# Linear attention and a squared-ReLU MLP on one core: the order of loads at the opening, and products, sums and sends at the very end

## The chip, the cores and the metric

The kernel runs on one core of a Trainium2 chip. The metric is the device time of one execution in microseconds, given as the median of several; lower is better. The profile shows one execution, whose span (first to last instruction) is a few microseconds shorter than the time.

The engines are named as the profile names them: PE is TensorE (PEld its weight loads), DVE is VectorE, ACT is ScalarE, POOL is GpSimd, SP is SyncE, which here only issues transfers. Each engine carries out its own instructions in the order in which the program emits them, and waits for other engines through semaphores.

## The reference

Linear attention over 8 batches, 8 heads, 576 positions and 64 features, then a two-layer MLP on the 4608 x 512 result:

```python
kv = np.einsum('bhsd,bhse->bhde', k, v)
out = np.einsum('bhsd,bhde->bhse', q, kv)
rms = np.sqrt(np.mean(out * out, axis=-1, keepdims=True) + 1e-06)
x = (out / rms * g_norm)          # then (B,H,S,D) -> (B*S, H*D)
h = x @ w_in                      # 512 -> 2048
r = np.maximum(h, 0.0)
return (r * r) @ w_out            # 2048 -> 512
```

q, k and v are float32. The two weight matrices come in 64 bits, and the kernel makes float32 of them itself.

## The kernel before

**Tiles and strips.** The 4608 rows of x are 36 tiles of 128 tokens; four tiles make a strip, so there are nine strips (s = 0 to 8). Each strip goes through an up-projection (`up_first` in strip 0, `up` later) and a down-projection (`down` in strips 0 and 1, `down_deep` from strip 2 on). From strip 1 on the matrix products are done by a scheme of seven products instead of eight on 2 x 2 blocks; `down_deep` uses it twice, so that each of its seven products p (in the order 4, 1, 2, 6, 5, 7, 3) is made of seven small products j.

**Attention as slices.** The attention of each batch is cut into small steps, the list `slices` (L487 to L512). `attend(n)` (L515) emits the steps up to number n; the main loop (L784 to L844) calls it between the MLP's products. So the attention of later batches is interleaved with the products of earlier strips, and only batch 0's first four tiles have to be done before anything else. That is the opening.

**The opening.** Heads go in pairs p = 0 to 3. For one pair the steps are: `convert_on_act(p)` (L199), the part of the conversion of a piece of W_in that runs on ACT (L203, L206); `transposed_query` (L318: four PE transposes L331, copied by ACT L333); `key_value` (L342: twenty matmuls L349, copied by ACT at L351 and L352); `first_queries(p)` (L415: the matmuls q times kv at L419, two DVE steps of the conversion of piece p, then `mean_squares`: ACT squares L384, DVE sums L386, L387); `first_normalized(p)` (L425: the third conversion step, the square root on ACT L392, DVE's reciprocal and one Newton step L393 to L398, the product x_n L430, the fourth conversion step); `first_features(p)` (L436: four PE transposes of x_n at L440, copied into xT by ACT at L441). `conversion` (L209) is the DVE part of a piece: four instructions, L215, L217, L221 and L224. Pair p's normalization and features follow pair p+1's queries and keys in the list. At the end of the opening `attend(ready[0] - 2)` (L780) emits all but the last pair's `first_normalized` and `first_features`; two more pieces, 4 and 5, then get their ACT part (L781, L782); then the main loop emits the last two steps.

All PSUM tiles of the attention come from one pool of four slots (`apsum`, L90).

**Loads of the opening.** All go from SP's queue in the order of L298 to L302: the rests of k and v, then in turn head pair p (k, v, and two transfers of q) and piece p of W_in (512 KB), then pieces up to the eighth. A piece is one of 32 parts of the two weight matrices (16 of W_in, 16 of W_out); pieces 0 to 3 hold the columns that strip 0 needs first. Eight buffers hold raw pieces; a buffer is loaded again when its piece has been converted. The rest of the conversion runs beside strip 0's up-projection (L588): `convert` (L280) emits the conversion of two pieces at a time, and ACT's part runs two pieces ahead.

**The end of a strip.** In `down_deep(s, k, i)` (L756), `small_products` (L723) emits the small products of product p: j = 1, 2, 3 for i = 0 and 4 to 7 for i = 1, each eight matmuls (L734). `PLACE` (L721) says to which of two PSUM tiles, and where in it, j is added: 1, 2 and 6 in the first; 5, 7, 3 and 4 in the second. `together(s, p)` (L739) makes the four quarters of p's result: an ACT copy of product 1 (L746), then four DVE sums (L745 is their line), then, for p = 2, 7 and 3, the sum with an earlier part and the sending of a finished block. It is emitted within the next product's steps, and for the last product (k = 6) at the very end. `send` (L652) sends a block of 256 tokens by 256 columns: two tiles, and for each of them the row groups of `out_rows` (L521). For batches from 2 on, a tile's 32-row groups go to rows that lie apart, so a tile takes four transfers, and a block eight, all from SP (L655).

Of the kernel before, what the change touches and what calls it, by code (L numbers as in the profile page):

```python
# [1 line left out]

# [17 lines left out]
def kernel(  # L20
# [34 lines left out]
    nc = tc.nc  # L55
    P = 128
    B, H, S, D = q.shape
# [3 lines left out]
    NP = H // 2  # L61
    FC = d_ff // P
    C = S // P
    REST = S - C * P
    PAIR = 2 * C + 1
    assert 2 * REST == P
    N_TILE = n_tok // P
    NT = 4
    STRIP = NT * P
    TH = STRIP // 2  # L70
    N_STRIP = N_TILE // NT
    DEEP = 2
    SQ = 32
    Q_ON_PE = 2
# [9 lines left out]
    small = ctx.enter_context(tc.tile_pool(name="small", bufs=3))  # L84
# [77 lines left out]
    def load_next(q_eng=nc.sync):  # L162
        u = next(to_load, None)
        if u is not None:
            load(*u, q_eng)


    KH, FH, DH = NP // 2, d_ff // 2, d_model // 2
    FQ = FC // 2
# [3 lines left out]
    w_in = wpool.tile([P, KH, NG, 7, WN // 2], FP32, name="w_in")  # L173
# [35 lines left out]
    def conversion(i, dest):  # L209

        c, r, high = words.pop(i)
        ci = c.bitcast(I32)


        yield nc.vector.tensor_scalar(out=c, in0=c, scalar1=LEAST, scalar2=MOST, op0=ALU.max, op1=ALU.min)  # L215

        yield nc.vector.tensor_scalar(  # L217
            out=ci, in0=ci, scalar1=3, scalar2=0x3FFFFFFF, op0=ALU.logical_shift_left, op1=ALU.bitwise_and
        )

        yield nc.vector.scalar_tensor_tensor(  # L221
            out=ci, in0=high, scalar=-(2**30), in1=ci, op0=ALU.bitwise_and, op1=ALU.bitwise_or
        )
        yield nc.vector.tensor_tensor(out=dest.bitcast(I32), in0=ci, in1=r, op=ALU.add)  # L224
# [69 lines left out]
    one = const.tile([P, 1], FP32, name="one")  # L294
# [1 line left out]
    nc.scalar.sqrt(one, one)  # L296

    load_rest(0, nc.sync)  # L298
    for p in range(NP):
        load_next()  # L300
        load_piece()
    load_more(0)  # L302
# [7 lines left out]
    flat = lambda t: t.rearrange("p h d -> p (h d)")  # L310
# [70 lines left out]
    def mean_squares(ps):  # L381
        n = ps.shape[-1] // D
        sq = xn_pool.tile([P, d_model], FP32, name="sq", tag="sq", bufs=1)
        nc.scalar.activation(sq, ps, AF.Square)  # L384
        ms = small.tile([P, H], FP32, name="ms", tag="ms")
        nc.vector.reduce_sum(out=ms, in_=by_head(sq), axis=AX.X)  # L386
        nc.vector.tensor_scalar(out=ms, in0=ms, scalar1=1.0 / D, scalar2=EPS, op0=ALU.mult, op1=ALU.add)  # L387
        return ms
# [23 lines left out]

    first = {}

    def first_queries(p):  # L415

        ps = apsum.tile([P, NT, P], FP32, name="x_ps", tag="at")
        for n in range(NT):
            nc.tensor.matmul(ps[:, n, :], lhsT=qT[0, p][:, n, :], rhs=kvd[0, p], start=True, stop=True)  # L419
        steps = conversion(p, w_in[:, p % KH, 0, p // KH * 2 : p // KH * 2 + 2])  # L420
        next(steps)
        next(steps)
        first[p] = flat(ps), mean_squares(flat(ps)), steps

    def first_normalized(p):  # L425
        ps, ms, steps = first.pop(p)
        next(steps)
        x_n["first", p] = t = xn_pool.tile([P, NT, P], FP32, name="x_n", tag="x_n")
        r = inverse_root(ms)
        nc.vector.tensor_tensor(  # L430
            out=by_head(flat(t)), in0=by_head(ps), in1=r.unsqueeze(2).to_broadcast([P, H, D]), op=ALU.mult
        )
        for _ in steps:
            pass

    def first_features(p):  # L436
        t, x = x_n.pop(("first", p)), open_xt(0)
# [47 lines left out]
        minus(nc.vector, t4, x(1, 0), t2)  # L485

    slices, ready = [], {}  # L487
    for b in range(B):
        for p in range(NP):
            if b:  # L490
                slices += [(transposed_query, (b, p)), (key_value, (b, p))]
                continue

            slices += [(convert_on_act, (p,)), (transposed_query, (b, p)), (key_value, (b, p))]
            if p > 0:
                slices.append((first_normalized, (p - 1,)))
            slices.append((first_queries, (p,)))
            if p > 0:
                slices.append((first_features, (p - 1,)))
        first_n = b // 2 * PAIR + (C if b % 2 else 0)  # L500
        ns = list(range(first_n, first_n + C + b % 2))
        if b == 0:
            slices += [(first_normalized, (NP - 1,)), (first_features, (NP - 1,))]
            ready[0] = len(slices)
            continue
        for i in range(len(ns) + 1):
            if i < len(ns):
                slices.append((query, (ns[i],)))
            if 0 < i <= len(ns):
                slices.append((features if b < X_ON_PE else squares_x, (ns[i - 1],)))  # L510
            if i > 0 and ns[i - 1] % NT == NT - 1:
                ready[ns[i - 1] // NT] = len(slices)  # L512
    slice_at = [0]

    def attend(n):  # L515
        while slice_at[0] < min(n, len(slices)):
            fn, a = slices[slice_at[0]]
            fn(*a)
            slice_at[0] += 1

    def out_rows(n):  # L521
        m, c = divmod(n, PAIR)
        if c == C:
            return [
                (slice(REST * h, REST * (h + 1)), out[(2 * m + h) * S + C * P : (2 * m + h + 1) * S, :])
                for h in range(2)
            ]
        b, c_b = (2 * m, c) if c < C else (2 * m + 1, c - C - 1)
        rows = out[b * S : b * S + C * P, :]
        if b < Q_ON_PE:  # L530
            return [(slice(0, P), rows.rearrange("(sp c) e -> c sp e", c=C)[c_b])]
        return [
            (ts(k, SQ), rows.rearrange("(i k) e -> k i e", k=4 * C)[4 * c_b + k]) for k in range(4)
        ]


    ORDER = (1, 2, 6, 5, 7, 3, 4)
# [87 lines left out]
    DEEP_ORDER = (4, 1, 2, 6, 5, 7, 3)  # L625
# [24 lines left out]
        return c_pool.tile([P, 2, DH], FP32, name="o_sb", tag="c")  # L650

    def send(s, th, eh, o):  # L652
        for t in range(2):
            for part, rows in out_rows(NT * s + 2 * th + t):
                nc.sync.dma_start(out=rows[:, ts(eh, DH)], in_=o[part, t, :])  # L655

    def down(s, p, i):
        if i == 0:
# [49 lines left out]
    leaf, chain, part = {}, {}, {}  # L708
# [11 lines left out]

    PLACE = {1: (0, 0), 2: (0, 1), 6: (0, 2), 5: (1, 0), 7: (1, 1), 3: (1, 2), 4: (1, 3)}  # L721

    def small_products(s, p, js):  # L723
        c = "B" if p in (4, 2, 5, 3) else "A"
        if js[0] == 1 and p not in (6, 7, 3):
            chain[c] = [
                fpsum.tile([P, 4, P], FP32, name=f"ps_{c}", tag=t, bufs=2 if t == "A" else 1)
                for t in ("AA" if c == "A" else "CB")
            ]
        for j in js:  # L730
            x, i = PLACE[j]
            a, w = leaf[p][j], w_blk.pop((s, p, j))
            for f in range(FQ // 2):
                nc.tensor.matmul(  # L734
                    chain[c][x][:, i, :], lhsT=a[:, f, :], rhs=w[:, f, :],
                    start=p not in (6, 7, 3) and j in (1, 3) and f == 0, stop=f == FQ // 2 - 1, skip_group_check=True,
                )

    def together(s, p):  # L739

        x, y = chain["B" if p in (4, 2, 5, 3) else "A"]
        o = part[p] = out_tile()
        q = o.rearrange("p t (h e) -> p (t h) e", h=2)
        one = lambda t: t.to_broadcast([P, 2, P])
        add = lambda out, a, b: nc.vector.tensor_tensor(out=out, in0=a, in1=b, op=ALU.add)  # L745
        nc.scalar.copy(q[:, 3], x[:, 0])  # L746
        add(q[:, 1:3], one(q[:, 3:4]), x[:, 1:3])
        add(q[:, 0:4:3], one(q[:, 2:3]), y[:, 0:2])
        add(q[:, 2], q[:, 3], y[:, 0])
        add(q[:, 0:4:3], q[:, 0:4:3], y[:, 2:4])  # L750

        for a, th, eh in {2: [(1, 0, 0)], 7: [(4, 1, 0), (5, 1, 1)], 3: [(6, 0, 1)]}.get(p, []):
            add(part[a], part[a], o)
            send(s, th, eh, part[a])

    def down_deep(s, k, i):  # L756
        p = DEEP_ORDER[k]
        small_products(s, p, ((1, 2, 3), (4, 5, 6, 7))[i])
        stream()
        q11, q12, q21, q22 = (gq[s, q] for q in (11, 12, 21, 22))  # L760
        if i == 1:
            if k == 0:
                nc.vector.tensor_tensor(out=q22, in0=q12, in1=q22, op=ALU.add)
            if k == 6:
                together(s, p)
            return
        if k:
            together(s, DEEP_ORDER[k - 1])
        if k == 1:
            minus(nc.vector, q12, q11, q12)  # L770
        if k == 2:
            minus(nc.vector, q11, q22, q11)
        if k == 4:
            minus(nc.vector, q21, q21, q11)
        if k < 6:
            leaf_sums(s, DEEP_ORDER[k + 1])
        if k == 6 and s + 1 < N_STRIP:
            sums_x(s + 1)

    attend(ready[0] - 2)  # L780
    for i in range(NP, NP + 2):  # L781
        convert_on_act(i)  # L782
    acted[0] = NP + 2
# [91 lines left out]
```

## Time and profile before

| | |
|---|---|
| time, median of 3 | 960.08 us (959.51 to 960.16) |
| span of the profiled execution | 956.8 us |
| PE busy | 924.3 us, 97% of the span |
| PE weight loads busy | 819.2 us, 86% |
| DVE busy | 670.8 us, 70% |
| ACT busy | 231.0 us, 24% |
| mean granted TensorE clock | 0.995 |
| DMA queue of SP | 184.86 MB, 60.7% of 16 engines |
| first matmul of the first strip (L588) | 37.92 us from the start |
| last matmul ends | 947.91 us |

In the profile's groups of instructions, a line gives the source line, engine, operation and tile, how often it ran, its busy time and mean duration, and the idle time before it with the instruction that ended it. The chain of work that ended last is followed back from the last instruction: each piece has its start, its length and what ran. A transfer appears twice: as the issue on SP's queue ("SPq"), and as the time from issue to landing. Times within the span are microseconds from its start.

### The profile page before, as it was taken

The page shows a single profiled execution, that of the slowest core. Times are in us where ns is not written, and L with a number is a line of the kernel's source. Part 1 is how long each engine was busy: PE and PEld are TensorE (multiplying, and loading weights), DVE is VectorE, ACT ScalarE, POOL GpSimd, SP SyncE. Part 2 cuts the span into 40 slices and gives each one's busy share as a digit, 9 for nine tenths or more (in the row PEclk, how much of TensorE's full clock was granted, in tenths as well). Part 3 has the DMA queues.
Part 4 walks back from the last instruction along what each step waited for, and adds up shares of the span by engine and source line. Part 5 has one row for each costly group of instructions (what it writes and reads, how often), then busy time and mean ns, then how long its engine had stood idle before and what let it go on. Part 6 is the DMA issues. An engine that isn't in the chain of part 4 may idle for free.

```text
span 956.8 us, 15744 instructions
## 1 busy us (share of the span) xinstructions
PE 924.3 (97%) x6144; PEld 819.2 (86%) x6144; DVE 670.8 (70%) x1217; ACT 231.0 (24%) x508; POOL 1.7 (0%) x7
## 2 busy tenths in 40 slices
PE   4699999999999999999999999999999999999996
PEld 4344888888888998899989998999889988998996
DVE  3899864585437995589648974797569755983594
ACT  3698441320023002210222012201320022002200
POOL 0000000000000000000000000000000000000000
PEclk9999999999999999999999999999999999999998
DMA  8699884536974585548563765478507721771074
GB/s 253 216 286 308 274 221 153 134 110 210 316 247 125 197 304 173 130 161 299 201 157 118 287 238 151 108 262 286 136 23 272 255 91 56 265 259 61 16 274 140
DMA packets 165530, 185.86 MB, mean 194 GB/s; under 512 B 85200, under 2 KB 138960, under 8 KB 156880
## 3 DMA queue, kind: packets, MB, share of 16 engines
q1 hardware_dynamic: 165296, 184.86, 60.7%
q8 instruction: 48, 0.79, 0.3%
q14 instruction: 26, 0.21, 0.1%
q10 hardware_dynamic: 160, 0.00, 0.0%
HBM read 153.62 MB, written 31.20 MB: 193 GB/s over the span
## 4 chain that ended last, share of the span: by engine, by line
PE 95%; ACT 2%; DVE 1%; DMA 1%; SPq 0%; issue 0%; DVEq 0%
PE ps_A L552 29%; PE ps_B L734 18%; PE ps_B L552 14%; PE ps_A L734 14%; PE ps_C L552 7%; PE ps_A L588 3%; PE x_ps L378 3%; PE kv_ps L349 2%; PE ps_C L588 1%; PE ps_B L588 1%; DMA raw<-in_moe_w_in_dram 1%; PE x_ps L419 0%; PE x_ps L373 0%; ACT raw L206 0%; PE xt_ps L440 0%
## 5 line engine op out<-in xcount | busy, mean ns | idle before, releaser
L552 PE MATMUL ps_A<-x_t,w_in 128*128 128x256 f32 x768 | 182.6, 381 | 1.3 <-DVE gt L611 1.3
L552 PEld LDWEIGHTS ps_A<-x_t,w_in 128*128 128x128 f32 x768 | 143.6, 190 | 21.1 <-DVE gt L611 2.1
L734 PE MATMUL ps_B<-w_blk,g_s 128*128 128x128 f32 x896 | 109.2, 275 | 0.0
L734 PEld LDWEIGHTS ps_B<-w_blk,g_s 128*128 128x128 f32 x896 | 104.6, 192 | 0.0
L734 PE MATMUL ps_B<-w_blk,gt 128*128 128x128 f32 x672 | 84.2, 275 | 0.0
L734 PE MATMUL ps_A<-w_blk,g_s 128*128 128x128 f32 x672 | 81.9, 275 | 0.0
L734 PEld LDWEIGHTS ps_B<-w_blk,gt 128*128 128x128 f32 x672 | 80.1, 192 | 0.4
L734 PEld LDWEIGHTS ps_A<-w_blk,g_s 128*128 128x128 f32 x672 | 78.4, 192 | 0.0
L612 DVE SCALAR_TENSOR_TENSOR gt<-gt 128x512 f32<-128x512 f32 x96 | 66.4, 692 | 3.3
L562 ACT COPY snap<-ps_A 128x512 f32<-128x512 f32 x68 | 39.8, 585 | 113.6 <-PE ps_A L552 98.8
L611 DVE TENSOR_TENSOR gt<-ps_C,snap 128x512 f32<-128x512 f32 x32 | 22.0, 688 | 62.7 <-PE ps_C L552 62.7
L611 DVE TENSOR_TENSOR gt<-ps_A,snap 128x512 f32<-128x512 f32 x32 | 22.0, 688 | 61.5 <-PE ps_A L552 61.3
L734 PE MATMUL ps_A<-w_blk,gt 128*128 128x128 f32 x504 | 63.1, 275 | 0.0
L552 PE MATMUL ps_A<-xT,w_in 128*128 128x256 f32 x256 | 61.2, 382 | 0.0
L552 PE MATMUL ps_C<-xT,w_in 128*128 128x256 f32 x256 | 61.0, 381 | 0.0
L241 DVE TENSOR_TENSOR gt<-gt 128x2048 f32<-128x2048 f32 (+1 forms) x31 | 58.1, 1874 | 4.0 <-PE ps_C L552 3.8
L552 PE MATMUL ps_B<-x_t,w_in 128*128 128x256 f32 x256 | 60.9, 381 | 0.0
L552 PE MATMUL ps_B<-xT,w_in 128*128 128x256 f32 x256 | 60.7, 380 | 0.0
L734 PEld LDWEIGHTS ps_A<-w_blk,gt 128*128 128x128 f32 x504 | 59.7, 192 | 0.0
L552 PEld LDWEIGHTS ps_C<-xT,w_in 128*128 128x128 f32 x256 | 48.1, 190 | 6.7 <-issue 0.2
L552 PEld LDWEIGHTS ps_B<-xT,w_in 128*128 128x128 f32 x256 | 48.3, 190 | 6.5
L552 PEld LDWEIGHTS ps_B<-x_t,w_in 128*128 128x128 f32 x256 | 48.1, 190 | 6.5
(117 smaller groups left out, 1213.9 us busy)
## 6 DMA issues: line engine op xcount, KB each, us to landing
w_blk<-w_deep SPq DMA_DIRECT2D x49, 1024.0 KB, 5.2
w_blk<-w_out SPq DMA_DIRECT2D x49, 768.0 KB, 5.2
w_blk<-w_out SPq DMA_DIRECT2D x11, 1024.0 KB, 6.9
raw<-in_moe_w_in_dram SPq DMA_DIRECT2D x16, 512.0 KB, 6.2
raw<-in_moe_w_out_dram SPq DMA_DIRECT2D x16, 512.0 KB, 5.7
k<-in_k_dram SPq DMA_DIRECT2D x30, 256.0 KB, 3.1
v<-in_v_dram SPq DMA_DIRECT2D x30, 256.0 KB, 3.6
w_deep<-w_t SPq DMA_DIRECT2D x7, 1024.0 KB, 9.0
```

Of the source, the lines that this page charges most:

```text
L241: eng.tensor_tensor(out=out, in0=a, in1=b, op=ALU.subtract)
L349: nc.tensor.matmul(ps[ts(h, D)], lhsT=a, rhs=w, start=c == 0, stop=c == C)
L378: nc.tensor.matmul(o, lhsT=qT[b, p][:, c_b, :], rhs=kvd[b, p], start=True, stop=True)
L552: nc.tensor.matmul(bank[BANK[p]][:, i, :], lhsT=lhsT(k), rhs=rhs(k), start=p in (1, 5, 2) and i == 0 and k == 0, stop=k == n - 1, skip_gro ...
L562: nc.scalar.copy(snap[p], b)
L588: nc.tensor.matmul(ps, lhsT=w_in[:, kc % KH, g, kc // KH * 2 + fh, ts(i, P)], rhs=xt[0][:, :, kc, :], start=kc == 0, stop=kc == NP - 1,)
L611: nc.vector.tensor_tensor(out=o, in0=b, in1=a, op=ALU.add)
L612: nc.vector.scalar_tensor_tensor(out=o, in0=o, scalar=0.0, in1=o, op0=ALU.max, op1=ALU.mult)
L734: nc.tensor.matmul(chain[c][x][:, i, :], lhsT=a[:, f, :], rhs=w[:, f, :], start=p not in (6, 7, 3) and j in (1, 3) and f == 0, stop=f == F ...
```

## The change

There are three parts.

**Opening, loads and steps.** Head pairs 0 and 1 are loaded before piece 0 of W_in; from then on pairs and pieces alternate as before, with pieces one pair later. The list of batch 0's steps is written out by hand: ACT's part of piece p now comes after pair p's queries instead of ahead of pair p's transposes; the DVE steps of the conversion are steps of their own (`piece`, with a count), placed between others; and all of batch 0's steps are emitted before pieces 4 and 5 get their ACT part. It is for ACT and DVE to meet the pair's own work first and the weights after it.

**The very end, products and sums interleaved.** In the last strip, products p = 5 and p = 3 (which share two PSUM tiles) place product 1, 3 and 4 in one tile and 2, 6, 5, 7 in the other. For the last product, p = 3, all seven small products are emitted in the order 1; then 2, 6, 5, 7; then 4, 3; and the steps of `together`, now a generator, come between: the copy of product 1, then the sums over 2, 6, 5, 7 together with the sum with part 6, then the last sum, over 3 and 4. It is for most of the sums to lie beside PE's last products.

**Sends.** `out_rows` returns groups of rows of two tiles, so that a block of batches from 2 on takes four transfers instead of eight; this holds in all strips. The very last block's transfers go in turn from SP and from ACT.

```diff
     load_rest(0, nc.sync)
-    for p in range(NP):
+    load_next()
+    for p in range(1, NP):
         load_next()
         load_piece()
     load_more(0)
...
-        steps = conversion(p, w_in[:, p % KH, 0, p // KH * 2 : p // KH * 2 + 2])
-        next(steps)
-        next(steps)
-        first[p] = flat(ps), mean_squares(flat(ps)), steps
+        first[p] = flat(ps), mean_squares(flat(ps))
...
+    act, T, K, Q, N, F, piece = (
+        convert_on_act, transposed_query, key_value, first_queries, first_normalized, first_features, first_piece
+    )
+    slices += [(T, (0, 0)), (K, (0, 0)), (Q, (0,)), (act, (0,))]
+    slices += [(T, (0, 1)), (K, (0, 1)), (piece, (0, 2)), (N, (0,)), (Q, (1,)), (act, (1,)), (piece, (0, 2))]
+    slices += [(T, (0, 2)), (K, (0, 2)), (piece, (1, 2)), (N, (1,)), (Q, (2,)), (F, (0,)), (act, (2,)), (piece, (1, 2))]
+    slices += [(T, (0, 3)), (K, (0, 3)), (piece, (2, 2)), (N, (2,)), (Q, (3,)), (F, (1,)), (piece, (2, 1)), (N, (3,))]
+    slices += [(act, (3,)), (F, (2,)), (piece, (2, 1)), (piece, (3, 4)), (F, (3,))]
+    ready[0] = len(slices)
...
+            cs = slice(c_b, c_b + (1 if t or c_b == C - 1 else 2))
+            both = slice(t, t + cs.stop - cs.start)
+            rows = out[b * S : b * S + C * P, :]
+            if b < Q_ON_PE:
+                to.append((slice(0, P), both, rows.rearrange("(sp c) e -> sp c e", c=C)[:, cs]))
+            else:
+                rows = rows.rearrange("(i c k) e -> k i c e", c=C, k=4)
+                to += [(ts(k, SQ), both, rows[k, :, cs]) for k in range(4)]
...
     def send(s, th, eh, o):
-        for t in range(2):
-            for part, rows in out_rows(NT * s + 2 * th + t):
-                nc.sync.dma_start(out=rows[:, ts(eh, DH)], in_=o[part, t, :])
+        for i, (part, t, rows) in enumerate(out_rows(NT * s + 2 * th)):
+            eng = nc.scalar if i % 2 and s == N_STRIP - 1 and (th, eh) == (0, 1) else nc.sync
+            eng.dma_start(out=rows[:, :, ts(eh, DH)], in_=o[part, t, :])
...
+    LAST_PLACE = {1: (1, 0), 2: (0, 0), 6: (0, 1), 5: (0, 2), 7: (0, 3), 3: (1, 1), 4: (1, 2)}
+    place = lambda s, p: LAST_PLACE if s == N_STRIP - 1 and p in (5, 3) else PLACE
...
-        nc.scalar.copy(q[:, 3], x[:, 0])
-        add(q[:, 1:3], one(q[:, 3:4]), x[:, 1:3])
-        add(q[:, 0:4:3], one(q[:, 2:3]), y[:, 0:2])
-        add(q[:, 2], q[:, 3], y[:, 0])
-        add(q[:, 0:4:3], q[:, 0:4:3], y[:, 2:4])
+        yield nc.scalar.copy(q[:, 3:4], small(1))
+        add(q[:, 1:3], one(q[:, 3:4]), small(2, 2))
+        add(q[:, 0:4:3], one(q[:, 2:3]), small(5, 2))
+        add(q[:, 2:3], q[:, 3:4], small(5))
+
+        if p == 3:
+            add(o, o, part[6])
+        yield
+        add(q[:, 0:4:3], q[:, 0:4:3], small(3, 2))
+        if p == 3:
+            send(s, 0, 1, o)
...
+        if s == N_STRIP - 1 and k == 6 and i == 1:
+
+            steps = together(s, p)
+            for js in ((1,), (2, 6, 5, 7), (4, 3)):
+                small_products(s, p, js)
+                next(steps)
+            return
...
-    attend(ready[0] - 2)
+    attend(ready[0])
```

More of the change, by code (lines that the diff above doesn't have):

```diff
@@ L1 @@
+from collections import deque
 from contextlib import ExitStack
@@ L419, in first_queries @@
             nc.tensor.matmul(ps[:, n, :], lhsT=qT[0, p][:, n, :], rhs=kvd[0, p], start=True, stop=True)
-        steps = conversion(p, w_in[:, p % KH, 0, p // KH * 2 : p // KH * 2 + 2])
-        next(steps)
-        next(steps)
-        first[p] = flat(ps), mean_squares(flat(ps)), steps
+        first[p] = flat(ps), mean_squares(flat(ps))
     def first_normalized(p):
-        ps, ms, steps = first.pop(p)
-        next(steps)
+        ps, ms = first.pop(p)
         x_n["first", p] = t = xn_pool.tile([P, NT, P], FP32, name="x_n", tag="x_n")
@@ L432, in first_normalized, with first_piece @@
         )
-        for _ in steps:
-            pass
+    first_steps = {}
+    def first_piece(i, n):
+        if i not in first_steps:
+            first_steps[i] = conversion(i, w_in[:, i % KH, 0, i // KH * 2 : i // KH * 2 + 2])
+        for _ in range(n):
+            next(first_steps[i])
     def first_features(p):
@@ L487 @@
     slices, ready = [], {}
-    for b in range(B):
-        for p in range(NP):
[L490 to L499, printed above, removed]
+    act, T, K, Q, N, F, piece = (
[7 more added lines that the diff above has]
+    ready[0] = len(slices)
+    for b in range(1, B):
+        for p in range(NP):
+            slices += [(transposed_query, (b, p)), (key_value, (b, p))]
         first_n = b // 2 * PAIR + (C if b % 2 else 0)
         ns = list(range(first_n, first_n + C + b % 2))
[L502 to L505, printed above, removed]
         for i in range(len(ns) + 1):
@@ L521, in out_rows @@
     def out_rows(n):
[L522 to L534, printed above, removed]
+        to = []
+        for t in range(2):
+            m, c = divmod(n + t, PAIR)
+            b, c_b = (2 * m, c) if c < C else (2 * m + 1, c - C - 1)
+            if c == C:
+                for h in range(2):
+                    rows = out[(2 * m + h) * S + C * P : (2 * m + h + 1) * S, :]
+                    to.append((slice(REST * h, REST * (h + 1)), slice(t, t + 1), rows.rearrange("p (t e) -> p t e", t=1)))
+                continue
+            if t and c_b > 0:
+                continue
+            cs = slice(c_b, c_b + (1 if t or c_b == C - 1 else 2))
[6 more added lines that the diff above has]
+                to += [(ts(k, SQ), both, rows[k, :, cs]) for k in range(4)]
+        return to
     ORDER = (1, 2, 6, 5, 7, 3, 4)
@@ L730, in small_products @@
         for j in js:
-            x, i = PLACE[j]
+            x, i = place(s, p)[j]
             a, w = leaf[p][j], w_blk.pop((s, p, j))
@@ L735, in small_products, with small @@
                     chain[c][x][:, i, :], lhsT=a[:, f, :], rhs=w[:, f, :],
-                    start=p not in (6, 7, 3) and j in (1, 3) and f == 0, stop=f == FQ // 2 - 1, skip_group_check=True,
+                    start=p not in (6, 7, 3) and j in ((1, 2) if place(s, p) is LAST_PLACE else (1, 3)) and f == 0, stop=f == FQ // 2 - 1, skip_group_check=True,
                 )
     def together(s, p):
-        x, y = chain["B" if p in (4, 2, 5, 3) else "A"]
+        def small(j, n=1):
+            x, i = place(s, p)[j]
+            return chain["B" if p in (4, 2, 5, 3) else "A"][x][:, i : i + n]
         o = part[p] = out_tile()
@@ L745, in together @@
         add = lambda out, a, b: nc.vector.tensor_tensor(out=out, in0=a, in1=b, op=ALU.add)
-        nc.scalar.copy(q[:, 3], x[:, 0])
-        add(q[:, 1:3], one(q[:, 3:4]), x[:, 1:3])
-        add(q[:, 0:4:3], one(q[:, 2:3]), y[:, 0:2])
-        add(q[:, 2], q[:, 3], y[:, 0])
-        add(q[:, 0:4:3], q[:, 0:4:3], y[:, 2:4])
-        for a, th, eh in {2: [(1, 0, 0)], 7: [(4, 1, 0), (5, 1, 1)], 3: [(6, 0, 1)]}.get(p, []):
+        yield nc.scalar.copy(q[:, 3:4], small(1))
[8 more added lines that the diff above has]
+            send(s, 0, 1, o)
+        for a, th, eh in {2: [(1, 0, 0)], 7: [(4, 1, 0), (5, 1, 1)]}.get(p, []):
             add(part[a], part[a], o)
             send(s, th, eh, part[a])
+        yield
     def down_deep(s, k, i):
         p = DEEP_ORDER[k]
-        small_products(s, p, ((1, 2, 3), (4, 5, 6, 7))[i])
+        if s == N_STRIP - 1 and k == 6 and i == 1:
[4 more added lines that the diff above has]
+            return
+        if s < N_STRIP - 1 or k < 6:
+            small_products(s, p, ((1, 2, 3), (4, 5, 6, 7))[i])
         stream()
@@ L764, in down_deep @@
             if k == 6:
-                together(s, p)
+                deque(together(s, p), 0)
             return
         if k:
-            together(s, DEEP_ORDER[k - 1])
+            deque(together(s, DEEP_ORDER[k - 1]), 0)
         if k == 1:
```

## The prediction

> **What bounds the kernel now.** I read the shares of the chain that ended last, then the busy time by stage, then that chain's pieces at both ends of the span.
>
> ```profile
> PE 95%; ACT 2%; DVE 1%; DMA 1%; SPq 0%; issue 0%; DVEq 0%
> ```
>
> ```profile
> 0.00:38.13 38.13, 17.16 (x145) 14.69 (x146) 18.63 (x49) 16.60 (x37) 1.70 (x7) 0.98 0.79 241
> 38.13:100.00 61.87, 61.87 (x230) 29.08 (x229) 59.95 (x135) 55.06 (x125) 0.00 (x0) 0.99 0.95 284
> 180.00:947.90 767.90, 765.94 (x5323) 706.43 (x5321) 542.50 (x938) 134.34 (x301) 0.00 (x0) 1.00 0.57 186
> 947.90:956.80 8.90, 0.00 (x0) 0.00 (x0) 1.82 (x4) 0.00 (x0) 0.00 (x0) 0.69 0.25 59
> ```
>
> Columns two to five after the length: PE, weight loads, DVE, ACT. PE is full from 38.13 to 947.90 us. The change leaves the number of products as it is, so it can win only in the first 38 us, where PE works 17, and in the last 8.9, where it works none. The second row warns: DVE, ACT and DMA are nearly full too while W is converted (38 to 100).
>
> The chain at the opening (start, length, what):
>
> ```profile
> 5.88 5.95 DMA raw<-in_moe_w_in_dram
> 12.42 0.66 ACT raw L206
> 13.08 0.47 ACT qT L333
> 14.01 2.06 PE x_ps L419 x8
> ...
> 33.04 0.55 ACT w_c L203
> 33.59 0.56 ACT raw L206
> 34.14 0.55 ACT w_c L203
> 34.69 0.54 ACT raw L206
> 35.23 0.10 ACT rms L392
> ...
> 37.01 1.12 PE xt_ps L440 x4
> 38.13 4.41 PE ps_A L588 x8
> ```
>
> ACT takes its queue in order: the first query copy (L333) stands behind piece 0's conversion and so behind its load; the last square root (L392) stands behind pieces 4 and 5, which nothing needs yet. The tail, by the chain and then by the timeline:
>
> ```profile
> 941.64 6.27 PE ps_B L734 x56
> ...
> 947.94 0.43 DVE o_sb L745
> ...
> 949.17 0.69 DVE o_sb L745
> ```
>
> ```profile
> 943.63 11.00 SPq L655 DMA_DIRECT2D out_dram<-o_sb  x24
> ```
>
> PE ends at 947.91 and DVE at 949.86, yet SP is still issuing: 24 sends at 0.458 us, the last eight (the last block's) after about 950.97. The last starts at 954.2; the span ends 2.6 later.
>
> **What the Trainium skill says.** "DMA: Bandwidth & Descriptors", Issuing engines are not separate DMA queues: sends from two engines share the same DMA engines, and only issue time is saved. Here issue time is what counts: the sends ran at some 70 GB/s. "PSUM — Partial Sum Buffer", PSUM bank collisions raise a hardware error: two engines must not be in one bank at once, so waits go by bank. The trace agrees: product 1's copy (L746) began at 947.04, when product 6, last of its bank, ended (48 of 56 matmuls), not when product 1 ended. "TensorE: Matmul & The Clock Gate", Part 1: PE runs at half clock until it has been busy for some 3.4 us. Here four query products took 2.04 us at 14 us and 1.16 at 24.
>
> **The change: opening.** No work is removed; order only. I lay it out by hand with the durations of the opening's timeline. ACT: copies 0.58 (the next starts 0.47 later), kv copies 0.2, square 0.60, the two conversion steps 0.66 each (0.56 apart), xT 0.69. DVE: sum 0.69, conversion 0.42, 0.43, 0.68, 0.68; square root to x_n's end 1.85.
> Loads: head pair 0 lands at 9.1, as before. One pair (768 KB) takes about 2.7 us and a piece 1.3 to 1.5, so piece 0 moves from 11.85 to about 14.5 (pair 1 landed at 14.6 with the same bytes ahead), pieces 1 and 2 to 18.6 and 22.7; pairs 1 to 3 come about 1.4 earlier (12.5, 17.3, 21.3).
> Pair 0: PE's transposes end at 10.3, key-values at 11.6; ACT copies qT at 10.35, kv by 12.05; queries (L419) start at 12.17 instead of 14.01; square 14.24, piece 0 on ACT 14.85 to 16.07.
> Pair 1: qT 15.97, kv to 16.87, queries 17.0 to 19.05 (18.70 before). DVE ends x_n(0) at 18.72.
> Pair 2: qT 20.77, kv to 21.67, queries 21.8 (24.44 before). DVE still finishes piece 0, so x_n(1) ends at 24.31; K(3) takes that PSUM slot and starts then.
> Pair 3: kv copied by 26.17, queries 26.3 (29.72 before); x_n(2) to 28.91; the last sum 28.95, square root 29.86, after conversion step 3 of piece 2 x_n(3) ends at 32.06. Its transposes start at 32.1, before at 37.01. Of these 4.9 us, 1.8 are from pair 0, 2.2 from pieces 4 and 5 leaving the front of the root, the rest from the shorter turns between.
> Piece 3 is ready at 34.75; the first strip asks for it 2.6 us after its start, at about 35.2. So PE's stream starts 4.9 us earlier, with a first group that may stay warm (3.43 instead of 4.41): up to 5.9.
>
> **What of it stays.** Conversion on DVE starts only at 34.75 for pieces 4 and 5, before at 37.48 (the row L215 x2): 2.7 earlier, less 0.1 for ACT; 2.6. From there DVE and ACT are full, so their end moves by 2.6 only. Who waits for that: x_ps L373, which needs the last copy of kv.
>
> ```profile
> 102.36 0.21 ACT L352 COPY kv_all<-kv_ps 64x64 f32<-64x64 f32 x1
> 103.33 1.09 PE L373 MATMUL x_ps<-kv_all,qT_rest 128*64 128x128 f32 x16
> ```
>
> There is 0.76 of slack between them, 0.13 of which the hand-over takes (13.87 to 14.01 at pair 0). The copy is behind the last pieces on ACT, whose load landed just in time (ACT waited 0.70 for it at 95.58, and SP sent it after DVE's stores). So the copy ends at about 99.97, and x_ps starts at 100.1: 3.2 to 3.3 us stay, the rest becomes a wait of PE of about 2 us there. Evacuations by ACT had at least 3.7 us of slack (a bank of step 2 emptied at 55.8, wanted at 59.54) and lose about 2.5: no wait. Opening: 3.3, from 2 (loads slow, piece 0 landing late) to 5.5 (DVE and ACT keep up).
>
> **The change: end.** In the last strip p=3 computes product 1, then 2, 6, 5, 7 into one bank, then 4 and 3 into the other. 16 of 56 matmuls follow 7: 1.79 us. In it DVE does three sums and the sum with part 6, 0.45 + 0.45 + 0.33 + 0.72 = 1.95 with gaps (rows of L745: 256, 256, 128 and 512 wide). It ends 0.2 after PE's end T; the last sum, 0.43, at T + 0.6. Before it was T + 1.95. ACT's copy of product 1 costs nothing: it lies under 2, 6, 5, 7. Queued behind DVE's waits is nothing but this chain; PE's 4 and 3 wait for a copy 3 us old. The leaf sums of p=3 were done at 940.06 and its last block issued at 935.42, so the new order of products meets no new wait.
> Sends: rows of two tiles in one transfer, four instead of eight per block. The page shows no issue of 32 partitions by two rows; the bounds are 0.42 (a send now) and 0.63 (W piece, 128 partitions by two rows). v, with 256 rows of 1 KB, takes 0.47. I take 0.47. The eight sends of p=7 take 3.8 and are done at 947.5 (at 0.63, 948.7), about when the last block is ready, T + 0.6 = 948.5. Then two on SP and two on ACT, which is idle: the last issue starts at T + 0.65 + 0.6 (ACT's two g_col issues took 1.20). From there 2.6 to the end as before, and 0.1 to 0.6 for twice the bytes, say 0.2. End: T + 4.1 to 4.4, before T + 8.89. Gain 4.6, from 3.5 to 5.
> In the other strips the sends lie under PE's stream: nothing. The two extra branches in Python cost nothing on the chip.
> Sum: 3.3 + 4.6 = 7.9; 960.1 - 7.9 = 952.2.
>
> **Rivals.** (a) The opening keeps its whole gain, 5 to 5.9: for it, the conversions have data (pieces 0 to 7 are loaded by 30 us and DMA idles until 40); against it, DVE's full row. 960.1 - 5.5 - 4.6 = 950.0. (b) The opening gives 1 or less: piece 0 lands after 15.5 and holds qT(1) behind it on ACT, or W's conversion is late by DMA (busy share over 1 from 60 to 80 us) and PE waits in the first strip; 960.1 - 0.8 - 4.6 = 954.7. (c) The tail gives less: two-row sends cost as much as two sends each, 0.9, p=7's eight hold SP until 950.8, or landing of 64 KB takes 2 us more: gain 2.5; 960.1 - 3.3 - 2.5 = 954.3. (d) Slower: the first strip's data or evacuations miss their turn so that PE cools and loses 4 to 6 us, more than the opening gives, and the last block waits for its weights, so that the tail gives 1 only: about 962. For it only that three engines are near full; nothing in the rows shows a load that close.
>
> **How the numbers follow.** The forecast 0.5, (a) 0.15, (b) 0.17, (c) 0.13, (d) 0.05. (a), (b) and (c) all lie within 949.5 to 955.8 with the bounds of the unknown costs; left out are (d) and the corners of two rivals at once. All but (d) and a small part of (b) with (c) are over 0.2% (1.9 us) faster: 0.94; same 0.03, slower 0.03.
>
> **What would show it.** First queries at about 12.2; x_n(3)'s transposes at 32; a new wait of PE at L373 near 98 to 100, for ACT's kv copy; DVE's conversions shifted by 2.6, not 5. At the end: one DVE sum after PE's last matmul, two sends on each of SP and ACT, the span ending 4.1 to 4.4 after PE. Wrong would be: PE waits in the first strip's L588 rows, piece 0 landing past 15.5, sends that take near 0.9 to issue.

## The result and the profile after

The changed kernel takes 951.53 us (median of 4 runs, 949.39 to 952.22) against 960.1 us. The ratio is 0.9908 (95% interval 0.9891 to 0.9926), so it is about 8.8 us faster, and between 7.1 and 10.5 (the two medians differ by 8.6). In a second set of runs the ratio was 0.9894 (0.9878 to 0.9910). The prediction was 952.2 us in a range of 949.5 to 955.8.

The shares of the chain that ended last, after:

```profile
PE 89%; DMA 4%; DVE 4%; ACT 1%; SPq 1%; issue 1%; DVEq 0%; ACTq 0%
```

Before, PE held 95% and DMA 1%. The busy time by stage shows why (length, then PE, weight loads, DVE, ACT, POOL, granted clock, DMA share, GB/s):

```profile
0.00:33.58 33.58, 16.80 (x145) 14.52 (x146) 16.54 (x45) 14.25 (x33) 1.70 (x7) 0.97 0.83 258
33.58:100.00 66.42, 66.31 (x257) 32.22 (x255) 63.46 (x142) 57.94 (x131) 0.00 (x0) 0.99 0.93 277
180.00:945.79 765.79, 764.01 (x5314) 704.59 (x5312) 541.67 (x938) 134.13 (x301) 0.00 (x0) 1.00 0.58 186
945.79:950.10 4.31, 0.00 (x0) 0.00 (x0) 0.66 (x2) 0.00 (x0) 0.00 (x0) 0.99 0.36 82
```

The stretch before the first strip is 4.5 us shorter and the tail 4.6 us, but PE's last product ends only 2.1 us earlier than before (945.79 against 947.89, the end of the last row of PE in each). These two gains, 2.1 and 4.6, make the 6.7 us by which the two profiled spans differ. That is less than the 8.6 to 8.8 us of the times, because the profiled execution of the kernel before took 958.59 us, less than any of those timed (959.51 to 960.16), and that of the changed kernel 951.91, a little over its median. So what is kept of the head start is probably more than this pair of profiles shows. The chain that ended last shows where the other 2.4 us of the head start went (start, length, what):

```profile
5.23 4.68 DMA q<-in_q_dram
13.07 2.06 PE x_ps L422 x8
...
32.47 1.12 PE xt_ps L446 x4
33.58 4.33 PE ps_A L599 x8
...
87.34 7.50 DMA raw<-in_moe_w_out_dram
...
101.70 0.22 ACT kv_all L354
101.96 0.43 PE x_ps L375 x2
```

The chain no longer runs through PE from 33.6 us on: it leaves it in the first strip and goes over a load of a piece of W_out, ACT's queue and the copy of kv to the product q times kv of the rest rows (L375; before, L373). ACT's and PE's rows there:

```profile
93.58 0.68 ACT L204 ACTIVATE w_c<-raw 128x512 f32<-128x512 f32 x1 [4.86 <-DMA raw<-in_moe_w_out_dram]
...
101.70 0.21 ACT L354 COPY kv_all<-kv_ps 64x64 f32<-64x64 f32 x1
```

```profile
100.19 0.43 PE L375 MATMUL x_ps<-kv_all,qT_rest 128*64 128x128 f32 x2 [0.31 <-ACT qT_rest L342]
101.96 0.43 PE L375 MATMUL x_ps<-kv_all,qT_rest 128*64 128x128 f32 x2 [1.33 <-ACT kv_all L354]
```

The brackets give the idle time and what ended it: 1.64 us of PE that the kernel before did not have here. The tail, by the chain and the timeline:

```profile
939.54 4.48 PE ps_B L748 x40
...
946.13 0.42 DVE o_sb L762
```

```profile
941.53 5.88 SPq L666 DMA_DIRECT2D out_dram<-o_sb  x10
...
946.63 0.85 ACTq L666 DMA_DIRECT2D out_dram<-o_sb  x2
```

Forty of the last 56 matmuls end at 944.02, the other sixteen beside DVE's sums; the last sum ends at 946.55, 0.76 after PE, and two sends leave from each of SP and ACT.

### The profile page after: what moved, and what is told of

Its sections match the earlier page's. It is cut to its first block, busy times and chain, and to the rows that moved or that the text cites. A ratio compares the mean times of both kernels' runs of the same rounds, so it can differ in the third digit from the quotient of the medians.

```text
span 950.1 us, 15646 instructions
## 1 busy us (share of the span) xinstructions
PE 924.9 (97%) x6144; PEld 819.0 (86%) x6144; DVE 671.0 (71%) x1217; ACT 230.7 (24%) x508; POOL 1.7 (0%) x7
## 4 chain that ended last, share of the span: by engine, by line
PE 89%; DMA 4%; DVE 4%; ACT 1%; SPq 1%; issue 1%; DVEq 0%; ACTq 0%
PE ps_A L563 28%; PE ps_B L748 18%; PE ps_A L748 14%; PE ps_B L563 13%; PE ps_C L563 7%; PE x_ps L380 3%; PE kv_ps L351 2%; DMA raw<-in_moe_w_out_dram 2%; PE ps_A L599 1%; DMA q<-in_q_dram 1%; DMA w_blk<-w_out 1%; PE ps_B L599 1%; DVE w_c L222 1%; DMA k_rest<-in_k_dram 1%; PE x_ps L422 0%
## 5 line engine op out<-in xcount | busy, mean ns | idle before, releaser
L388 DVE TENSOR_REDUCE ms<-sq 128x8 f32<-128x512 f32 x36 | 24.6, 684 | 44.2 <-ACT sq L386 43.6
```

## The experiments

All of them are read at four points: where the first strip starts (the first row of L588, before), how long its first group of eight matmul rows takes, where the rest rows' product ends, and how long the span goes on after PE's last row.

| kernel | start | first group | rest product ends | tail | PE's wait for W in strip 1 | ratio to before (95%) |
|---|---|---|---|---|---|---|
| before | 37.92 | 4.61 | 104.42 | 8.91 | 0 | 1 |
| whole change | 33.38 | 4.54 | 102.39 | 4.31 | 0.4 | 0.9908 (0.9891 to 0.9926) |
| whole change again | 32.39 | 4.73 | 100.96 | 4.28 | 0.3 | 0.9894 (0.9878 to 0.9910) |
| e1_opening | 32.05 | 5.81 | 101.71 | 8.88 | 2.8 | 0.9951 (0.9936 to 0.9965) |
| e2_end | 38.05 | 5.25 | 105.19 | 4.30 | 2.7 | 0.9954 (0.9939 to 0.9970) |
| e3_sums | 32.28 | 6.15 | 100.47 | 8.92 | 0.5 | 0.9951 (0.9934 to 0.9967) |
| e4_sends | 32.62 | 3.65 | 101.10 | 5.38 | 0.2 | 0.9919 (0.9903 to 0.9936) |
| e5_sp | 33.47 | 6.09 | 101.90 | 4.76 | 0.6 | 0.9908 (0.9896 to 0.9921) |
| e6_twelve | 32.52 | 5.93 | 100.34 | 4.26 | 2.5 | 0.9898 (0.9880 to 0.9915) |
| e8_steps | 33.66 | 6.07 | 101.62 | 4.27 | 2.1 | 0.9938 (0.9920 to 0.9956) |
| e8b_steps (same kernel) | 32.96 | 4.64 | 101.23 | 4.31 | 0 | 0.9906 (0.9893 to 0.9919) |
| e9_late | 33.57 | 5.74 | 101.20 | 4.30 | 0 | 0.9906 (0.9890 to 0.9921) |
| e12_warm | 34.44 | 3.60 | 100.92 | 4.28 | 0 | 0.9921 (0.9908 to 0.9934) |
| e13_warm8 | 35.21 | 3.60 | 105.75 | 4.29 | 0 | 0.9952 (0.9935 to 0.9970) |

The first columns are one execution each, the ratio is of several. PE's wait for blocks of W in strip 1's down-projection goes from 0 to 2.8 us from one execution to another: 2.1 and 0 in the same kernel (e8 and e8b), 2.8 with the opening alone, 2.7 with the end alone, 0 in the one profile of the kernel before. That sets how small a difference these times can show. The rest of the span is steady: from the end of the rest rows' product to PE's last row it is 842.6 to 843.5 us in every trace, once this wait and one wait for v near 280 us (1.6 us in e3, 0.9 in e12, 1.3 in e13) are taken off. Only e1 is longer, 845.2. The start of the first strip varies by about 1 us, and the traces show where that arises: pair 1's four query products took 2.08 us in the first profile of the change and in e5, e8, e9 and e13, and 1.16 in the others with the changed steps, and pair 2's queries came 4.7 us after them instead of 3.8 to 4.1. Why they differ is open.

### The parts apart: e1_opening and e2_end

The edits are the change's own hunks: for e1 the loads, the list of steps and `attend(ready[0])`; for e2 `out_rows`, `send`, `LAST_PLACE`, `small_products`, `together` and `down_deep`.

> The opening's part alone (loads and steps), with the end as before. Theory: the first strip starts 4.5 us earlier, but the conversion of W moves less, so PE's stream ends 2 to 3 us earlier: 957 to 958, with a wait of PE at the first product q times kv of the rest rows. Rival one, the whole head start stays: 955.5. Rival two, the opening gives nothing that lasts and the end does all: 960.

> The end's parts alone (sums and sends), the opening as before. Theory: 4.6 us by the span after the last matmul, 8.9 to 4.3: 955.5. If the parts are not additive (the end's gain partly from the opening's shift), 953 or 957.

The opening alone gives 0.9951, 4.7 us (3.4 to 6.2); the end alone 0.9954, 4.4 us (2.9 to 5.9). Together that is 9.1 us; the whole change gives 8.8 and 10.2 in its two sets of runs. So the parts add up within the noise, and e2's 955.63 us is the 955.5 expected. e1 came out faster than my expectation of 957 to 958, which I had taken from the first profile after the change (rest product at 102.39, the latest but for e13 of those with the changed steps). By the time alone, 955.96 us, it is nearer to the first rival (the whole head start stays, 955.5), and the interval of 3.4 to 6.2 us does not exclude it. Its profile does: the first strip starts 5.9 us earlier than before and the rest product ends only 2.7 us earlier. PE's wait there showed, as expected, 1.3 us for the copy of kv:

```profile
101.28 0.43 PE L374 MATMUL x_ps<-kv_all,qT_rest 128*64 128x128 f32 x2 [1.33 <-ACT kv_all L353]
```

This profile is of the slowest of e1's 14 executions, 960.41 us. It shows the path, not the gain: PE waited 2.8 us for W in strip 1, and after the longest of these waits (2.10 us) the granted clock was 0.74 and 0.50 (254 to 256 and 256 to 258 us).

### Sums without sends, sends without sums: e3_sums and e4_sends

e3 leaves the two-tile sends and the use of ACT's queue out of the whole change; e4 leaves the interleaving out:

```diff
-        for i, (part, t, rows) in enumerate(out_rows(NT * s + 2 * th)):
...
+        for t in range(2):
+            for part, rows in out_rows(NT * s + 2 * th + t):
```

and, e4 against the whole change:

```diff
-            for js in ((1,), (2, 6, 5, 7), (4, 3)):
...
-        if s < N_STRIP - 1 or k < 6:
-            small_products(s, p, ((1, 2, 3), (4, 5, 6, 7))[i])
+        small_products(s, p, ((1, 2, 3), (4, 5, 6, 7))[i])
```

> Opening, and products and sums interleaved at the end, but sends as before (a tile at a time, eight for a block, all from SP). Theory: SP is still sending the block before when the sums are done, so the interleaving alone gives nothing: the same as the opening alone to 0.3 us, the last send still starting some 10.5 us after SP's first of that batch. Rival, the sums are on the path: 1.2 to 1.5 us less than the opening alone.

> Opening, and sends of two tiles with the last block from SP and ACT, but products and sums not interleaved. Theory: now the sums end the path; the last block is ready 1.95 us after the last matmul instead of 0.75: 1.2 us slower than the whole change, 952.7. Rival, the sums hide behind the sends still: the same as the whole change, 951.5.

e3 has the ratio of the opening alone, 0.9951, and the same tail, 8.92. Its timeline says why (end of DVE's last sum; SP's sends):

```profile
945.82 0.42 DVE o_sb L754
```

```profile
941.21 11.00 SPq L658 DMA_DIRECT2D out_dram<-o_sb  x24
```

The block is ready at 946.24, but SP issues one send in 0.458 us and has 16 of them ahead of the last eight; it reaches those at about 948.5 and is busy until 952.21. Interleaving the sums alone wins nothing: it shortens a chain that was not the last to end. e4 has a tail of 5.38: with half the sends SP is done in time, and now the sums end last.

```profile
945.59 0.69 DVE o_sb L755
```

```profile
940.06 7.03 SPq L665 DMA_DIRECT2D out_dram<-o_sb  x10
...
946.36 0.84 ACTq L665 DMA_DIRECT2D out_dram<-o_sb  x2
```

The send of the last block starts with the end of DVE's sum (946.28), not after a queue. So of the end's 4.6 us the sends are worth 3.5 (8.9 to 5.4), and the interleaving 1.1 more, but only with them. Both expectations held by the traces; the times alone (e3 0.4 us under e1, e4 952.16) could not tell differences of this size.

### Which engine issues the last block: e5_sp

```diff
-            eng = nc.scalar if i % 2 and s == N_STRIP - 1 and (th, eh) == (0, 1) else nc.sync
-            eng.dma_start(out=rows[:, :, ts(eh, DH)], in_=o[part, t, :])
+            nc.sync.dma_start(out=rows[:, :, ts(eh, DH)], in_=o[part, t, :])
```

> The whole change, but the very last block's four sends all from SP. Theory (issue time on SP is on the path; four issues at 0.47 us instead of two on each engine): the last issue starts 0.9 us later and the span ends 0.9 later after the last matmul, 5.3 instead of 4.45 us. Rival (the DMA engines set the pace of the last sends, not the issuing engine): 4.45 as before.

```profile
940.98 6.84 SPq L665 DMA_DIRECT2D out_dram<-o_sb  x12
```

The tail is 4.76 instead of 4.28 to 4.31, so 0.46 longer: half of what I expected, neither theory in full. The last issue starts 0.9 us later than with two queues (947.39, 1.38 after the sum's end; in the whole change 0.49), but the sends then land faster: 1.7 us by the median with SP alone, 1.8 and 2.0 on SP and ACT together (one execution of e5; the second profile of the whole change and e4 have 1.8 and 2.0 too). ACT's queue is worth about half a microsecond, less than a run can tell (0.9908 again).

### What holds the copy of kv: e6_twelve

```diff
-    raw_pool = conv.enter_context(tc.tile_pool(name="raw", bufs=8))
+    raw_pool = conv.enter_context(tc.tile_pool(name="raw", bufs=12))
...
-        while len(raw) < min(end + 8, max(len(sources) - 4, end + 4), len(sources)):
+        while len(raw) < min(end + 12, max(len(sources) - 4, end + 8), len(sources)):
```

> The whole change again, beside the next three on the same chip: 8 to 9 us under the kernel before, ratio 0.991. The first strip starts near 33.5 us, and PE waits at the rest rows' first product (q times kv) near 100 us.

> The whole change with twelve buffers for raw pieces of W instead of eight, so that each piece is asked for four pieces earlier, the first ones in the gap in which DMA idled (27 to 40 us). Nothing else differs. Theory (the last pieces' loads hold ACT, ACT's queue holds the copy of kv, and that copy holds PE): ACT's waits for pieces of W_out (5.7 us in the change's profile) go, PE's wait at the rest rows' product goes with them, and 1 to 2 us are won: 950. Rival (DVE's conversion work itself is the bound): ACT's waits for loads go, but DVE is as late as before, PE still waits 1 us or more there, and the time is that of the whole change to 0.5 us.

ACT waits for no piece of W_out any more, and the copy of kv is ready before PE comes for it:

```profile
96.64 0.21 ACT L354 COPY kv_all<-kv_ps 64x64 f32<-64x64 f32 x1
```

```profile
99.25 1.09 PE L375 MATMUL x_ps<-kv_all,qT_rest 128*64 128x128 f32 x16
```

So the mechanism is shown: late pieces held ACT, ACT held the copy, the copy held PE. In eight executions with the changed steps and eight buffers (the whole change twice, e1, e3, e4, e5, e8b and e13) the rest product ends 0.47 to 0.48 us after the copy does; in e6, e8, e9 and e12 it ends 0.7 us or more after it, so there PE itself came last. The rival (DVE's work as the bound) fails in its reason: the last conversion step on DVE starts at 95.5 in e6, at 97.0 in the whole change beside it and at 99.6 before, so DVE could go earlier once the pieces were there. The rival's time is what was measured, though (950.66 against 950.24), and the gain of 1 to 2 us did not follow: the rest product ends at 100.34, 0.6 us earlier than in the whole change beside it (100.96), because PE itself came only at 99.25. Its first group had taken 5.93 us at a mean granted clock of 0.60, where the other took 4.73 at 0.76. In strip 1 the same execution then lost 2.5 us waiting for blocks of W. The ratio, 0.9898, is that of the whole change (0.9894).

### Is it the start that counts: e9_late

```diff
-    slices += [(T, (0, 3)), (K, (0, 3)), (piece, (2, 2)), (N, (2,)), (Q, (3,)), (F, (1,)), (piece, (2, 1)), (N, (3,))]
+    slices += [(T, (0, 3)), (K, (0, 3)), (piece, (2, 2)), (N, (2,)), (Q, (3,)), (F, (1,)), (piece, (2, 1)), (act, (4,)), (act, (5,)), (N, (3,))]
...
     attend(ready[0])
-    for i in range(NP, NP + 2):
-        convert_on_act(i)
```

> The whole change with ACT's part of pieces 4 and 5 put back ahead of the last head pair's square root. Theory (what the conversion of W allows sets what is kept of the head start): the first strip starts about 2 us later, near 35.5, but PE then finds the copy of kv ready near 100 us, its wait there is gone, and the time is within 0.7 us of the whole change. Rival (the start of the first strip sets the end): 2 us slower than the whole change.

```profile
33.57 5.74 PE L599 MATMUL ps_A<-xT,w_in 128*128 128x512 f32 x8
```

```profile
100.26 0.21 ACT L354 COPY kv_all<-kv_ps 64x64 f32<-64x64 f32 x1
```

```profile
100.11 1.09 PE L375 MATMUL x_ps<-kv_all,qT_rest 128*64 128x128 f32 x16
```

The start moves by 1.2 us against the whole change beside it (33.57 and 32.39), less than the 2 I expected. Of this 0.8 us is the edit: from pair 3's queries to the first strip it is 7.3 us here and 6.5 in the whole change, both times. The rest comes from the loads and queries ahead of that: pair 0's q came 0.6 earlier here, and pair 1's queries took 0.9 longer. With a first group of 5.74 us instead of 4.73, PE is 2.2 us behind after that group. Yet it finds the copy in time, and the rest product ends at 101.20, within 0.3 us. The ratio is within 0.12% of the whole change's. Over these 2 us the start of the first strip does not set the end of this stretch.

### The order of the loads: e8_steps and e8b_steps

```diff
     load_rest(0, nc.sync)
-    load_next()
-    for p in range(1, NP):
+    for p in range(NP):
         load_next()
         load_piece()
```

> The whole change with the loads in the order of before (piece 0 ahead of head pair 1); the list of steps as changed. Theory (the order of steps gives the head start, the loads only have to keep out of its way): head pair 0's q lands at 9.1 instead of 9.9, the first queries start at 12.2, pair 1's q lands at 14.6 just in time, and the first strip starts within 0.8 us of the whole change's 33.4, the time the same to 0.5 us. Rival (the loads' order matters): pair 1 comes late for PE, or piece 0 holds ACT, and the first strip starts 1.5 us or more later.

> The same kernel as e8_steps again, for a second profile: the new list of steps with the loads in the order of before. If the loss of 3 us seen there belongs to the loads' order, it shows again, 953 to 954, and the profile should show where between the first strip's start and strip 1. If it was chance (late weights in strip 1, a cold first group), the time is that of the whole change, 950 to 951.5.

The same kernel gave 0.9938 and 0.9906. The first start is at 33.66 and 32.96, within what the whole change itself shows (33.38 and 32.39), and the rest product ends at 101.62 and 101.23. The profile of the first set puts 2.1 us into strip 1's blocks of W, a wait that the second does not have. What the rival foretold also shows once, but small: in e8 PE waited 0.59 us for pair 1's q (at 15.17), in e8b and in the whole change not. The two sets ran on different chips, e8 beside the whole change (0.9894) and e8b beside e5 (0.9908), so it is likely, but not shown, that the loss of the first set was chance and not the loads' order. The order of the steps is enough for the head start.

### Two limits at once: e13_warm8 and e12_warm

PE's first group takes 3.6 us at full clock (3.65 in e4, at a granted clock of 1.00). I put filler matmuls into PE's two gaps ahead of the last two groups of transposes, with eight raw buffers (e13) and with twelve (e12):

```diff
+    def filler(n):
+        ps = apsum.tile([P, 4 * P], FP32, name="fill_ps", tag="at")
+        for _ in range(n):
+            nc.tensor.matmul(ps, lhsT=ident, rhs=flat(qT[0, 3]), start=True, stop=True)
...
-    slices += [(act, (3,)), (F, (2,)), (piece, (2, 1)), (piece, (3, 4)), (F, (3,))]
+    slices += [(act, (3,)), (filler, (2,)), (F, (2,)), (piece, (2, 1)), (piece, (3, 4)), (filler, (5,)), (F, (3,))]
```

> The whole change with seven filler matmuls of 128x512 (results not used) where PE idles ahead of the last two groups of transposes of the opening, to keep its clock up. Theory (with eight raw buffers the copy of kv sets the end of the stretch): the first group of the first strip takes about 3.5 us instead of 4.5 to 6, PE reaches the rest rows' product 1 to 2 us earlier, and waits there as much longer; time within 0.7 us of the whole change. Rival (PE's own stream sets it): 1 to 2 us won.

> The same filler matmuls with twelve raw buffers. Theory (two limits meet there: W's conversion, removed by the buffers, and PE's cold clock, removed by the filler): PE reaches the rest rows' product at 97 to 97.5, finds the copy of kv ready, and the stretch ends 1.5 to 2.5 us earlier than in the whole change: about 948.5. Rival (after the buffers something else, DVE's work or strip 1's weights, sets the end): 950 to 951, no better than the whole change.

PE in e12:

```profile
29.71 4.46 PE L496 MATMUL fill_ps<-qT,ident 128*128 128x512 f32 x10
...
34.44 3.60 PE L604 MATMUL ps_A<-xT,w_in 128*128 128x512 f32 x8
...
66.69 0.30 PE L339 MATMUL tr_ps<-ident,q_rest 128*128 128x128 f32 x1 [0.75 <-DMA q_rest<-in_q_dram]
```

Both theories failed (e12's rival, no better than the whole change, held), and the first reason is the filler: five matmuls are ten rows of the trace, 4.46 us, twice what I had reckoned, so the second filler outlasted the gap and the first strip started 1 to 3 us late. The clock did come (3.60 for the first group, at 1.00), and in e12 the two cancelled: the rest product ends at 100.92. PE also waited in this stretch for batch 1's own loads, 0.75 us for q's rest rows, a third limit; this wait is also in e4 (2.0) and e8b (1.0). e13 lost 4 to 6 us by its ratio: in its profile ACT waited 5.16 us for a piece, and PE 1.6 for q's rest rows, 0.8 for q, 1.3 for the copy and, after this stretch, 1.3 for v. Why the loads were that much later there than in the other kernels with eight buffers is not settled. What a warm start would be worth without its own cost stays open, and no kernel here beats the whole change by more than the noise.

## Why the prediction was right, and where its steps were off

**Opening, start of the first strip.** Foretold by the hand schedule: queries at 12.2, x_n(3)'s transposes at 32.1. Measured: 13.07 and 32.47. The first was off because pair 0's q came later (PE starts on it at 10.05, before at 9.25); e8 and e8b show 9.50 and 10.54 with the loads in the old order, so the order of the loads is not shown to be the cause. The turns between pairs absorbed half of it, as pairs 1 to 3 ran at 17.76, 22.48 and 26.86 where I had 17.0, 21.8 and 26.3. The transposes came 4.5 us earlier than before, foretold 4.9. Of these, 2.2 were to come from pieces 4 and 5 leaving the front of the root; e9, which puts them back, is later by only 0.8, so that term was too large.

**First group warm.** I had left open that it might take 3.43. It took 3.65 in e4 and 4.5 to 6.2 in the other kernels without filler (rows of the timeline, 0.2 longer than the chain's 3.43 and 4.41); the optimistic end of rival (a) needed the warm one.

**What of it stays.** The step was: DVE and ACT are full, so the conversion moves by 2.6 us only, PE will wait at the rest rows' product for the copy of kv, and 3.3 us stay. The wait came at that line, for that copy, and e6 showed its cause by taking it away. The wait of "about 2 us" was 1.64. Its reason was half right. What held ACT was not that DVE and ACT were full, but that the last pieces landed late. The prediction had named a wait of 0.70 us for the last of these loads and passed over the one just before it:

```profile
93.64 0.67 ACT L203 ACTIVATE w_c<-raw 128x512 f32<-128x512 f32 x1 [2.80 <-DMA raw<-in_moe_w_out_dram]
```

The conversion of pieces 4 and 5 began at 35.28 (the first L216 after piece 3), 2.2 us earlier than before, and SP asked for the last piece at 87.3, also 2.2 earlier. But ACT could go on with the last two pieces only at 93.58 and 94.93, where before it was 93.64 and 95.58, so the copy of kv came 0.7 us earlier (101.70 against 102.36) and not the 2.6 foretold. In the second profile it came 2.1 earlier (100.27).

Kept were 2.0 us in the first profile and 3.5 in the second (104.42 to 102.39 and 100.96), and 2.5 to 4.1 in the other kernels with the changed steps, e13 apart. These are counted from one execution of the kernel before; e2, with the old opening, ends its rest product at 105.19, which would make each 0.8 more. By the times the opening is worth 4.7 us (3.4 to 6.2, e1), more than the 3.3 foretold. So the mechanism of the wait was right; that the size fell inside the range owes something to luck, since it hangs on when the last loads land, and nothing in the prediction's working let that vary. Nor had I seen that batch 1's own loads bind in this stretch too.

**The end.** Foretold 4.1 to 4.4 us after PE; measured 4.31. Eight sends of p=7 in 3.8, the new send at 0.47: 10 sends took 5.88 with a wait in it, and the median issue is 0.427, no dearer than the one-tile send (0.419). The last sum at T + 0.6; measured 0.76, since DVE began 0.09 later than product 7's end and then ran 1.93 + 0.09 + 0.42. The gain was 4.60, foretold 4.6. Here the prediction did not say which of the two parts gives what; e3 and e4 do.

**The rivals.** (a), the whole head start kept, fell by the traces, not by the time (its 950.0 us lies inside the interval): every kernel with the changed steps but e13 ends the stretch at 100.3 to 102.4, whether the first strip starts at 32.1 or at 34.4. One support that it had was misread: DMA did not idle from 30 to 40 us before, its share was 0.34. (b) and (c) fell in their main point, since the opening kept over 2 us and the sends got no dearer. Of (d) one piece exists, PE waiting for data in the first strip and in strip 1, but at 1 to 3 us, in some executions, and in strip 1 with the old opening as well (in e2, 2.7).

## What to carry to other kernels

A head start is worth only what the next stream that cannot move lets through: before adding up a gain at the opening, look for the first place where the two meet (here PE meets ACT's queue, which stands behind weight loads), and take every wait in that queue from the trace, not only the last. At the end of a kernel count the issues still queued on the sending engine: a chain of sums is not worth shortening while the queue is behind it, and becomes worth it as soon as the queue is shorter. When a wait is removed, look at once for the next two within a microsecond of it.

## What was not expected of the hardware

A send of 32 partitions by two rows of 1 KB took 0.427 us to issue (median), one of 32 by one row 0.419: twice the bytes at nearly the same issue time. Landing of the last block's four sends was slower when they came from two queues (1.8 and 2.0 us) than from one (1.7, one execution), so splitting the issues gave back half of what it saved. The same kernel gave ratios of 0.9938 and 0.9906 in two sets of runs on two chips, with intervals that barely miss each other (0.9920 to 0.9956, 0.9893 to 0.9919): in this kernel differences under 0.3% need more than one set.
